# An FFT convolution and an MLP on one core: the filter loaded already turned, angle sums on GpSimd, fewer and wider shift matmuls, a new planned order

## The chip, the core and the metric

The kernel runs on one core of a Trainium2 chip. The metric is the device time of one execution in microseconds; several executions are run and the median is taken. The profiled execution is a single one of them, and its span is the time from its first to its last instruction.

TensorE (PE) multiplies, VectorE (DVE), ScalarE (ACT) and GpSimd (POOL) work on vectors, and SyncE (SP) issues most of the transfers (DMA). Each engine takes its instructions strictly in the order in which the program wrote them.

## The reference

Sequence length S = 2048, width D = 512, batch 1, bf16. A convolution block is followed by an MLP block, each with a residual. Layer norms have no weights.

```python
k_shift = sum over t of shift(k, 3 - t) * shift_k[:, t]       # 4 taps along the sequence
kv = k_shift * v
y  = irfft(rfft(kv, padded to 4096) * rfft(ssm_k, padded to 4096))[:2048] + kv * ssm_D
h  = q + layernorm(q) * y
# mixer and MLP on B = layernorm(h)
g  = gelu(layernorm(B) @ w1)              # then its four column groups move by -1, +1, -2, +2 rows
x1 = B + moved(g) @ w2
out = h + x1 + gelu(layernorm(x1) @ w3) @ w4    # w3: 512 x 1792, w4: 1792 x 512
```

## The kernel before

**Data.** Row `16 p + b` of the sequence lies in partition `p`, block `b` (16 blocks of 128 rows). The transforms of length 4096 are done as matmuls in two steps. A first small transform (`step1`, table `f1`) works on four blocks at once. Then an exchange over SBUF by DMA brings the rows together, and a second transform (`step2`, table `ftab`) follows for each of 16 frequency groups `kh`. Each group is multiplied by the filter's spectrum, transformed back (`inverse`), and sent over SBUF again; the last transform back (`inv1`) opens the MLP.

**Two plans.** The program is written as a list of tasks. A class `Plan` gives each task a cost on one or more engines, simulates them, tries 40 sets of priorities with random steps, and emits the best order it found. The numbers in it are a guess that sets the order and nothing else. There is one plan for the convolution and one for the MLP. Task names that are used below:

- `h`, `k`, `v`, `q`: loads of the filter (4 pieces), of k (4 pieces, transposed by the DMA), of v and of q (2 pieces of 1 MB each).
- `T`, `TE`: the filter comes as 512 x 2048 into `hnat`; `T` turns 128 x 128 pieces on PE, and `TE` copies them into `xh`. `dr` adds `ssm_D` to the filter's first row.
- `F`, `FE`, `FX`: first transform of the filter (tile `ph`, 16 tiles), its copy out of PSUM, and its exchange (L401, 16 transfers).
- `S`, `X`: the four shifted taps of k as matmuls against diagonal matrices `diag` (tile `pk`, 8 tiles of 128 x 1024), and the product with v on DVE (tile `xk`).
- `K`, `KE`, `KX`: first transform of kv (tile `pc`), its copy, its exchange (16 transfers).
- `G`, `GE`: second transform of the filter and its copy. `W`, `A`: second transform of kv (tile `pw`) and its copy. `P`: two products on DVE (L531, L532). `V`, `VE`, `VX`: transform back (tile `pv`), copy and exchange.
- `uu`, `an`, `sn`, `sg`, `tg`: the angles of the table `ftab` as integer sums, their wrap to 12 bits, the sines on ACT, signs, and the edges on POOL. `B`, `BE`: transposed tables for the way back. `diag`: the diagonal matrices, on POOL.
- `qs`, `qn`: statistics of q's rows for its layer norm (16 of them), and the power -1/2 on POOL.
- In the MLP: `I` is the last transform back (L598), `Y` scales it on ACT (L609), `H` forms h and its statistics on DVE (L620, L615), `W`, `X`, `M`, `O` are the four matmuls w1 to w4.

All PSUM tiles of the convolution come from one pool of four buffers (`big`): the n-th tile that PE fills waits until the tile four places ahead of it has been copied out. Copies out of PSUM (`FE`, `KE`, `GE`, `VE`) go to ACT or DVE, whichever the plan chose. All copies are written by one helper and so have line L321 (ACT) or L323 (DVE).

Of the kernel before, what the change touches and what calls it, by code (L numbers as in the profile page):

```python
# [34 lines left out]
class Plan:  # L35
# [26 lines left out]
    def forward(self, prio):  # L62
# [6 lines left out]
        while ready:  # L69
# [79 lines left out]
def kernel(  # L149
# [19 lines left out]
    KW = 16 + S  # L169

# [11 lines left out]
    hnat = view(ra, 0, DC * S, "p (c n) -> p c n", c=DC)  # L182
# [13 lines left out]
    ui = rt[:, 0:NK * 2 * 32].bitcast(I16)  # L196
# [14 lines left out]
    dum = const.tile([P, 1], F32, name="dum")  # L211
# [66 lines left out]
    a1 = small.tile([P, NK], I16, name="a1")  # L278
    b2i = small.tile([P, 2, 32], I32, name="b2i")
    b2 = small.tile([P, 2, 32], I16, name="b2")  # L280
# [27 lines left out]
    plan = Plan({"big": 4, "xk": 4, "asb": 3, "pr": 4, "vst": 5}, 40, {"V": 5.6, "A": 6.2, "G": 2.8, "PE": 5.5, "D": 1.8})  # L308
# [18 lines left out]

    def load(o, i, transpose=False):
        return lambda e: (nc.sync.dma_start_transpose if transpose else nc.sync.dma_start)(o, i)
# [10 lines left out]
    def angles(e):  # L340
        for r in range(2):
            nc.vector.tensor_tensor(out=uu[:, :, r, :, :],  # L342
                                    in0=a1[:].rearrange("p (k t) -> p k t", t=2).unsqueeze(3).to_broadcast([P, NH, 2, 32]),
                                    in1=b2[:, r, :].unsqueeze(1).unsqueeze(1).to_broadcast([P, NH, 2, 32]), op=ADD)
# [25 lines left out]
    task(("uu",), {"V": 2.4}, angles)  # L370
    task(("an",), {"V": 0.7}, wrap, [("uu",)])
    task(("sn",), {"A": 2.0}, sines, [("an",)])
    task(("sg",), {"V": 0.75}, signs, [("sn",)])
    task(("tg",), {"G": 2.3}, edges, [("sg",)])
    task(("diag",), {"G": 4.2}, taps, [("an",)])

    def turn(c, g):
        def f(e):
            pt = big(("pt", c, g), dt=BF16)
            for j in range(8):  # L380
                nc.tensor.transpose(pt[:, j, :], hnat[:, c, 8 * g + j:S:16], ident[:])
        return f

    def turned(c, g):
        return lambda e: copy(e, xh[:, 8 * g:8 * g + 8, c * P:(c + 1) * P], tl["pt", c, g])
# [9 lines left out]
    def out1(key, zc, bl, h):  # L395
        return lambda e: copy(e, zc[:, bl, h, :, :], tl[key][:])
# [7 lines left out]
    for g in range(2):  # L404
        for c in range(DC):
            task(("T", c, g), {"PE": 0.6}, turn(c, g), [("h", c)], take="big")
            task(("TE", c, g), {"A": 0.95, "V": 0.64}, turned(c, g), drop=("T", c, g))
    task(("dr",), {"V": 0.4}, lambda e: nc.vector.tensor_tensor(out=xh[0:1, 0, :], in0=xh[0:1, 0, :], in1=drow[:], op=ADD),
         [("TE", c, 0) for c in range(DC)])
    for bl in range(NL):  # L410
        for h in range(4):
            task(("F", bl, h), {"PE": 0.56}, step1(("ph", bl, h), lambda bq, bl=bl: xh[:, 4 * bl + bq, :], h),
                 [("TE", c, bl // 2) for c in range(DC)] + [("dr",)], take="big")
# [3 lines left out]
    def shift(p):  # L417
        def f(e):
            pk = big(("pk", p))
            for i in range(2):  # L420
                b = 2 * p + i
                for c in range(DC):
                    for j in range(4):
                        nc.tensor.matmul(pk[:, i, c * P:(c + 1) * P], lhsT=kT[:, c, 16 + b - j:KW - 16 + b - j + 1:16],  # L424
                                         rhs=diag[:, c, j, :], start=(j == 0), stop=(j == 3))
        return f

    def gated(p):
        def f(e):
            if p % 2 == 0:  # L430
                tl["xk", p // 2] = xkp.tile([P, 4, D], BF16, name="xk", tag="xk")
            nc.vector.tensor_tensor(out=tl["xk", p // 2][:, 2 * (p % 2):2 * (p % 2) + 2, :], in0=tl["pk", p][:],  # L432
                                    in1=v_sb[:, 2 * p:2 * p + 2, :], op=MUL)
        return f

    for p in range(NB // 2):
        task(("S", p), {"PE": 2.3}, shift(p), [("k", c) for c in range(DC)] + [("diag",)] + ([("S", p - 1)] if p else []), take="big")
        task(("X", p), {"V": 1.25}, gated(p), [("v", p // 4)] + ([("X", p - 1)] if p % 2 else []), take=None if p % 2 else "xk",
             drop=("S", p))
    for bl in range(NL):  # L440
        for h in range(4):
            task(("K", bl, h), {"PE": 0.56}, step1(("pc", bl, h), lambda bq, bl=bl: tl["xk", bl][:, bq, :], h),
                 [("X", 2 * bl + 1)], take="big", drop=("X", 2 * bl))
            task(("KE", bl, h), EV, out1(("pc", bl, h), zck, bl, h),
                 [("F", 3, 3)] if bl > 1 else [("T", c, 1) for c in range(DC)], drop=("K", bl, h))
# [58 lines left out]
    def qnorm(e):  # L504
        nc.gpsimd.tensor_scalar(out=qrs[:], in0=qmv[:, :, 1], scalar1=1e-5, scalar2=1.0, op0=ADD, op1=MUL)
        nc.gpsimd.tensor_tensor(out=qrs[:], in0=qrs[:], in1=mhalf[:, 0:1].to_broadcast([P, NB]), op=OP.pow)

    for b in range(NB):
        task(("qs", b), {"V": 0.85}, qstat(b), [("q", b // 8)])
    task(("qn",), {"G": 3.3}, qnorm, [("qs", b) for b in range(NB)])  # L510
    for kh in range(NH):
        task(("G", kh), {"PE": 0.56}, step2(("pg", kh), zh, kh), [("FX", bl) for bl in range(NL)] + [("tg",)], take="big")
# [5 lines left out]
    turns = {"asb": 0, "pr": 0, "vst": 0}  # L518
# [65 lines left out]
    plan = Plan({"mm": 6, "pt": 2, "lb": 6, "z": 4})  # L584
# [192 lines left out]

    for b in range(NB):
        if b % 4 == 0:
            task(("I", b // 4), {"PE": 2.45}, inv1(b // 4), take="mm", many=4)  # L780
        task(("Y", b), {"A": 0.72}, gate(b), take="z", drop=("I", b // 4), part=b % 4)
        task(("H", b), {"V": 1.6}, hsum(b), drop=("Y", b))
        if b % 2:
# [62 lines left out]
```

## Time and profile before

| what | value |
|---|---|
| median of 3 runs | 254.23 us (254.24, 254.23, 253.06) |
| profiled execution, its time | 252.79 us |
| its span | 251.0 us, mean granted clock 0.973 |
| busy: PE, DVE, ACT, POOL | 224.1, 165.0, 135.7, 54.0 us |
| instructions | 4538 |

The page of the profile has the busy share of each engine in 40 slices, the chain of work that ended last, the costliest groups of instructions and the transfers. Rows of a timeline give start, total duration, engine, line, operation, tile written and tiles read, the count, and in brackets the idle time ahead of it with what ended it. A duration is from an instruction's start to its end; neighbours overlap a little, so the pace of a row of equal instructions is a little shorter than one duration. Rows of windows give, after the stretch and its length, busy time and count for PE (and, where no engine is chosen, PE's weight loads, DVE, ACT and POOL), then the granted clock, the share of DMA and GB/s.

### The profile page before, as it was taken

Reading aid. Unit: us, or ns where it says so; the run is one execution under the profiler, and the core shown is the slowest. Engines: PE = TensorE matmul, PEld = TensorE weight load, DVE = VectorE, ACT = ScalarE, POOL = GpSimd, SP = SyncE. Lnnn points to the kernel's source line nnn. Section 1 sums busy time; section 2 is a strip of 40 time slices with the busy share of each in tenths; the row PEclk is TensorE's granted clock in tenths of the full one; section 3 lists DMA queues with packets and bytes.
Section 4 is the critical chain, followed back from the end, with each engine's and each line's share of the span. In section 5 each row is a group of like instructions: output and inputs, shape, how many; then the busy total and the mean of one; then the engine's idle time right before and its main releaser. Section 6 shows DMA issues by size and latency. Waiting matters only on the chain.

```text
span 251.0 us, 4538 instructions
## 1 busy us (share of the span) xinstructions
PE 224.1 (89%) x1803; PEld 118.6 (47%) x1803; DVE 165.0 (66%) x325; ACT 135.7 (54%) x191; POOL 54.0 (22%) x101
## 2 busy tenths in 40 slices
PE   8489998987988966388899999999999999999994
PEld 3446985443332322165567564454444444444441
DVE  7979899997997955999999947991222320015221
ACT  3567018877997995579379565567000067641000
POOL 3630000005010020699974522420000000000000
PEclk9959999999999999979799999999999999999999
DMA  6999980586245287900000000000011100000111
GB/s 219 263 237 411 376 341 4 230 356 252 102 139 198 101 264 242 379 7 4 0 0 3 0 1 3 1 0 0 24 42 42 42 24 0 0 21 24 42 42 42
DMA packets 18791, 28.08 MB, mean 112 GB/s; under 512 B 10065, under 2 KB 13906, under 8 KB 17234
## 3 DMA queue, kind: packets, MB, share of 16 engines
q1 hardware_dynamic: 17952, 26.74, 30.6%
q0 software_dynamic: 288, 1.05, 1.4%
q8 instruction: 14, 0.23, 0.4%
q10 hardware_dynamic: 530, 0.01, 0.1%
q14 instruction: 7, 0.06, 0.1%
HBM read 11.02 MB, written 2.10 MB: 52 GB/s over the span
## 4 chain that ended last, share of the span: by engine, by line
PE 58%; DVE 26%; ACT 5%; POOL 4%; DMA 3%; issue 2%; SPq 1%; ACTq 0%; POOLq 0%
PE mm L766 19%; PE mm L751 19%; PE mm L711 5%; PE pk L424 3%; DVE ra L323 3%; DVE qst L500 3%; DVE rd L620 3%; DVE st L615 3%; PE mm L686 2%; DVE xk L432 2%; DVE rt L342 2%; ACT rb L321 2%; DVE rb L531 2%; PE ptx L672 2%; DVE rb L532 2%
## 5 line engine op out<-in xcount | busy, mean ns | idle before, releaser
L757 ACT ACTIVATE ra<-mm 128x512 bf16<-128x512 f32 x56 | 33.4, 597 | 49.7 <-PE mm L751 49.6
L774 DVE TENSOR_TENSOR ob<-mm,rd 128x512 bf16<-128x512 f32 x16 | 11.1, 692 | 61.4 <-PE mm L766 61.4
L751 PE MATMUL mm<-rc,rb 128*128 128x512 bf16 x224 | 50.8, 379 | 0.0
L766 PE MATMUL mm<-rt,ra 128*128 128x512 bf16 x224 | 49.0, 379 | 0.0
L766 PEld LDWEIGHTS <-ra 128*128 128x128 bf16 x224 | 21.9, 98 | 26.4
L751 PEld LDWEIGHTS <-rb 128*128 128x128 bf16 x224 | 21.7, 98 | 24.8
L321 ACT CAST rc<-ph 128x1024 bf16<-128x1024 f32 x11 | 10.8, 1025 | 15.0 <-PE ph L392 15.0
L541 PE MATMUL pv<-rb,rt 64*128 64x512 bf16 x128 | 16.6, 378 | 2.0 <-DVE rd L323 1.3
L686 PE MATMUL mm<-rc,rf 128*128 128x256 bf16 x128 | 17.8, 294 | 0.0
L711 PE MATMUL mm<-rf,rb 128*128 128x512 bf16 x64 | 16.9, 391 | 0.4 <-ACT rb L692 0.3
L321 ACT CAST rb<-pw 128x1024 bf16<-128x1024 f32 x16 | 16.2, 1027 | 2.1 <-PE pw L454 1.4
L424 PEld LDWEIGHTS <-rb 128*128 128x128 bf16 x256 | 16.3, 149 | 1.5 <-issue 1.5
L424 PE MATMUL pk<-diag,rb 128*128 128x128 bf16 x256 | 16.6, 226 | 0.3 <-ACT ra L321 0.3
L321 ACT COPY rc<-ptx 128x512 bf16<-128x512 bf16 x26 | 14.7, 587 | 3.9 <-PE ptx L672 3.9
L620 DVE SCALAR_TENSOR_TENSOR rd<-q_sb,qmv,z 128x512 bf16<-128x512 bf16 x16 | 12.7, 791 | 6.0 <-ACT z L609 6.0
L716 DVE SCALAR_TENSOR_TENSOR q_sb<-rd,cr,mm 128x512 bf16<-128x512 bf16 x16 | 11.7, 734 | 4.2 <-PE mm L711 4.2
L686 PEld LDWEIGHTS <-rf 128*128 128x128 bf16 x128 | 13.2, 106 | 2.2
L692 ACT ACTIVATE rb<-mm 128x512 bf16<-128x512 f32 x16 | 9.5, 610 | 7.4 <-PE mm L711 5.3
L609 ACT ACTIVATE z<-mm,qrs 128x512 f32<-128x512 f32 x16 | 10.6, 697 | 4.4 <-PE mm L598 2.7
L321 ACT CAST rb<-pv 128x1024 bf16<-128x1024 f32 x12 | 12.1, 1039 | 1.3 <-PE pv L541 1.3
L454 PEld LDWEIGHTS <-rf 128*64 128x64 bf16 x128 | 6.6, 108 | 13.0 <-issue 9.4
L640 POOL TENSOR_TENSOR rr<-uw,mhalf 128x4 f32<-128x4 f32 x8 | 10.4, 1296 | 10.3 <-DVE hm L629 10.3
(128 smaller groups left out, 333.7 us busy)
## 6 DMA issues: line engine op xcount, KB each, us to landing
rd<-rc SPq DMA_DIRECT2D x16, 256.0 KB, 4.9
rc<-ra SPq DMA_DIRECT2D x16, 256.0 KB, 3.4
ra<-rb SPq DMA_DIRECT2D x16, 256.0 KB, 2.7
ra<-in_A_ssm_k_dram SPq DMA_DIRECT2D x4, 512.0 KB, 5.2
q_sb<-in_A_q_dram SPq DMA_DIRECT2D x2, 1024.0 KB, 7.7
rb<-in_A_v_dram SPq DMA_DIRECT2D x2, 1024.0 KB, 10.6
out_dram<-ob SPq DMA_DIRECT2D x16, 128.0 KB, 1.8
rb<-in_B_w_dram SPq DMA_DIRECT2D x1, 1792.0 KB, 7.0
```

The source lines that it names most:

```text
L321: nc.scalar.copy(o, i)
L424: nc.tensor.matmul(pk[:, i, c * P:(c + 1) * P], lhsT=kT[:, c, 16 + b - j:KW - 16 + b - j + 1:16], rhs=diag[:, c, j, :], start=(j == 0), st ...
L541: nc.tensor.matmul(ps[:, t, :], lhsT=tt[hs, min(x, 2), kh, :], rhs=pr[hs, x // 2, x % 2, :], start=(x == 0), stop=(x == 3))
L609: nc.scalar.activation(z[:], tl["y", b][:], ACT.Identity, bias=1.0, scale=qrs[:, b:b + 1])
L620: nc.vector.scalar_tensor_tensor(out=h_sb[:, b, :], in0=q_sb[:, b, :], scalar=qmv[:, b, 0:1], in1=tl["z", b][:], op0=SUB, op1=MUL)
L686: nc.tensor.matmul(pw_[:, j * 256:(j + 1) * 256], lhsT=w1_sb[:, k, m * P:(m + 1) * P], rhs=hnT[:, k, p * 256:(p + 1) * 256], start=(k == 0 ...
L711: nc.tensor.matmul(px[:], lhsT=shifted(m, b), rhs=w2_sb[:, m, :], start=(m == 0), stop=(m == DC - 1))
L716: nc.vector.scalar_tensor_tensor(out=x1[:, b, :], in0=hbm[:, b, :], scalar=tl["cr", b // 2][:, b % 2:b % 2 + 1], in1=tl["x", b][:], op0=MU ...
L751: nc.tensor.matmul(pg[:], lhsT=w3_sb[:, k, fc * P:(fc + 1) * P], rhs=lnT[:, k, g * 512:(g + 1) * 512], start=(k == 0), stop=(k == DC - 1))
L757: nc.scalar.activation(gbuf[:, g % 2, fc, :], tl["g", g, fc][:], ACT.Gelu_apprx_tanh)
L766: nc.tensor.matmul(po[:], lhsT=gbuf[:, g % 2, fc, i * P:(i + 1) * P], rhs=w4_sb[:, fc, :], start=(fc == 0), stop=(fc == FC - 1))
L774: nc.vector.tensor_tensor(out=ob[:], in0=tl["o", 4 * g + i][:], in1=xh1[:, b, :], op=ADD)
```

## The change

- The host hands the filter over turned and laid out as 128 x 16 x 512; it is loaded straight into `xh`. `T` and `TE` are gone.
- All twelve loads are issued in one written order: the filter's four pieces, k 0 and 1, v 0 and 1, q 0, k 2 and 3, q 1.
- The angle sums `uu` move from DVE to POOL and to int32, behind two copies of 8 columns into `dumg`, which wait for the tables `f1` and `s0`. The wrap (now int32) and the sines are written behind the fourth copy that DVE makes of `ph`, the signs and edges behind the fifth.
- `S` is cut by four blocks and two column groups: 14 matmuls of 128 to 512 columns into one tile, against 32 of 128 columns.
- Ten statistics of q stay in the convolution's plan, six move to the front of the MLP's, with a second power on POOL.
- Dummy matmuls `wm` on zeros: three tiles at the end of the first plan, behind VE 13 to 15, and four in the second, behind H 2 to 5.
- The planner frees a tile that has no reader, tries 150 sets of priorities in place of 40, and has smaller PE costs; a task `in` of 3.4 stands ahead of `I`.

```diff
-    ui = rt[:, 0:NK * 2 * 32].bitcast(I16)
+    ui = rt[:, 0:NK * 4 * 32].bitcast(I32)
...
-    for c in range(DC):
-        task(("h", c), {"D": 1.45}, load(hnat[:, c, :], A_ssm_k[c * P:(c + 1) * P, :]), lat=LAND, rank=60)
+    for bl in range(NL):
+        task(("h", bl), {"D": 1.45}, load(xh[:, 4 * bl:4 * bl + 4, :], A_ssm_k[:, 4 * bl:4 * bl + 4, :]), lat=LAND, rank=60)
...
     def angles(e):
-        for r in range(2):
-            nc.vector.tensor_tensor(out=uu[:, :, r, :, :],
+        for r in range(-2, 2):
+            if r < 0: nc.gpsimd.tensor_copy(dumg[:], (f1[:, 3, 1, 24:32], s0[:, 1, 1, 24:32])[r]); continue
+            nc.gpsimd.tensor_tensor(out=uu[:, :, r, :, :],
...
     def out1(key, zc, bl, h):
-        return lambda e: copy(e, zc[:, bl, h, :, :], tl[key][:])
+        def f(e):
+            copy(e, zc[:, bl, h, :, :], tl[key][:])
+            if e == "V" and key[0] == "ph":
+                turns["rc"] = turns.get("rc", 0) + 1
+                for g in {4: (wrap, sines), 5: (signs, edges)}.get(turns["rc"], ()):
+                    g(e)
+        return f
...
-            pk = big(("pk", p))
+            pk = big(("pk", bl, ch))
             for i in range(2):
-                b = 2 * p + i
-                for c in range(DC):
-                    for j in range(4):
-                        nc.tensor.matmul(pk[:, i, c * P:(c + 1) * P], lhsT=kT[:, c, 16 + b - j:KW - 16 + b - j + 1:16],
-                                         rhs=diag[:, c, j, :], start=(j == 0), stop=(j == 3))
+                c = 2 * ch + i
+                for m in (0, -3, -2, -1, 1, 2, 3):
+                    lo, hi, x = max(0, -m), min(3, 3 - m), 16 + 4 * bl + m
+                    nc.tensor.matmul(pk[:, i, P * (m + lo):P * (m + hi + 1)], lhsT=kT[:, c, x:x + S - 15:16],
+                                     rhs=diag[:, c, lo:hi + 1, :].rearrange("p j x -> p (j x)"), start=(m == 0), stop=(m == 3))
...
-    for b in range(NB):
+    for b in range(NQ):                      # NQ = 10
         task(("qs", b), {"V": 0.85}, qstat(b), [("q", b // 8)])
...
+    for kh in range(NH - 3, NH):
+        task(("wm", kh), {"PE": 0.87}, warm, [("VE", kh)], take="big", rank=-10)
+    for n in (0, 1, 2, 3, 4, 5, 8, 9, 10, 6, 7, 11):
+        loads[n]()
...
+    task(("in",), {"D": 3.4}, lambda e: None)
+    for b in range(NQ, NB):
+        task(("qs", b), {"V": 0.85}, qstat(b), rank=20)
+    task(("qn",), {"G": 1.7}, qnorm(NQ, NB), [("qs", b) for b in range(NQ, NB)])
...
+        if 1 < b < 6:
+            task(("wm", b), {"PE": 0.87}, warm(b), [("H", b)], take="mm", rank=-100)
...
+        if name == "A_ssm_k":
+            a = _np.ascontiguousarray(a.T.reshape(P, NB, D))
```

DVE, from the angle table `u0k` to the first statistics of q, before:

```order
L303 TENSOR_SCALAR u0k<-u0k 128x128
L342 TENSOR_TENSOR rt<-a_161,b_163 128x16x64 x2
L323 COPY ra<-pt 128x8x128
L347 TENSOR_SCALAR rt<-rt 128x2048
L323 COPY ra<-pt 128x8x128 x3
L408 TENSOR_TENSOR ra<-ra,drow 1x512
L353 TENSOR_SCALAR rf<-rf,sgo 128x64x32
L323 CAST rc<-ph 128x1024 x5
L500 BN_STATS qst<-q_sb 128x6
```

and after the change (`rt` holds the angles, `rf` the table, `ra` the filter, `rc` its first transform):

```order
L305 TENSOR_SCALAR u0k<-u0k 128x128
L407 TENSOR_TENSOR ra<-ra,drow 1x512
L325 CAST rc<-ph 128x1024 x4
L353 TENSOR_SCALAR rt<-rt 128x2048
L325 CAST rc<-ph 128x1024
L359 TENSOR_SCALAR rf<-rf,sgo 128x64x32
L432 TENSOR_TENSOR xk<-pk,rb 128x4x256 x3
```

The sums and the four copies of turned pieces have left DVE; the added row is its first work on data, and the wrap stands behind four copies of F and ahead of the fifth.

POOL, from its last small constant to the edges of the table, before:

```order
L251 MEMSET u0p 128x1
L366 TENSOR_TENSOR diag<-ident,ssk_bf 128x2048
L356 TENSOR_SCALAR rf<-s_181,pf 128x2x32
L357 TENSOR_SCALAR rf<-s_181,pf 128x2x32
L358 COPY t_72<-rf 128x2x127
```

and after:

```order
L253 MEMSET u0p 128x1
L347 COPY dumg<-f_70 128x8
L347 COPY dumg<-s_182 128x8
L348 TENSOR_TENSOR rt<-a_162,b_164 128x16x64 x2
L372 TENSOR_TENSOR diag<-ident,ssk_bf 128x2048
L362 TENSOR_SCALAR rf<-s_182,pf 128x2x32
```

Two small copies and the two sums now stand ahead of the diagonal matrices. SP's queue of loads, as one piece of the difference:

```order
-L329 DMA ra<-in_A_ssm_k_dram 128x2048 x4
-L329 DMA_TRANSPOSE rb<-in_A_k_dram 128x2048 x4
-L329 DMA q_sb<-in_A_q_dram 128x4096
-L329 DMA rb<-in_A_v_dram 128x4096
+L333 DMA ra<-in_A_ssm_k_dram 128x2048 x4
+L333 DMA_TRANSPOSE rb<-in_A_k_dram 128x2048 x2
+L333 DMA rb<-in_A_v_dram 128x4096 x2
+L333 DMA q_sb<-in_A_q_dram 128x4096
+L333 DMA_TRANSPOSE rb<-in_A_k_dram 128x2048 x2
```

The second half of k's transposed pieces now stands behind both pieces of v and the first of q.

More of the change, by code (lines that the diff above doesn't have):

```diff
@@ L96, in forward @@
                     gone[m, i] = done[n] + t["lat"]
+            if t["take"] and not any(t["users"]):
+                gone.update({(n, i): done[n] for i in range(t["many"])})
             ready.remove(n)
@@ L368, in taps @@
                                 in1=ssk_bf[:].rearrange("p c j -> p (c j)").unsqueeze(2).to_broadcast([P, 16, P]), op=MUL)
[L370 to L374, printed above, removed]
-    task(("diag",), {"G": 4.2}, taps, [("an",)])
[L377 to L385, printed above, removed]
+    task(("uu",), {"G": 5.0}, angles)
+    turns = {"asb": 0, "pr": 0, "vst": 0}
+    task(("an",), {"V": 2.2}, lambda e: None, [("uu",)])
+    task(("sn",), {"A": 2.0}, lambda e: None, [("an",)])
+    task(("sg",), {"V": 0.75}, lambda e: None, [("sn",)])
+    task(("tg",), {"G": 2.3}, lambda e: None, [("sg",)])
+    task(("diag",), {"G": 4.2}, taps, [("an",)])
     def step1(key, xs, h):
@@ L440 @@
+    for bl in range(NL):
+        for ch in range(2):
+            task(("S", bl, ch), {"PE": 1.78}, shift(bl, ch), [("k", 2 * ch), ("k", 2 * ch + 1), ("diag",)], take="big")
+            task(("X", bl, ch), {"V": 1.25}, gated(bl, ch), [("v", bl // 2)] + ([("X", bl, 0)] if ch else []), take=None if ch else "xk",
+                 drop=("S", bl, ch))
     for bl in range(NL):
         for h in range(4):
[L442 to L443 removed]
+            task(("K", bl, h), {"PE": 0.45}, step1(("pc", bl, h), lambda bq, bl=bl: tl["xk", bl][:, bq, :], h),
+                 [("X", bl, 1)], take="big", drop=("X", bl, 0))
```

79 lines of the change are left out of this document (43 added, 36 removed).

## The prediction

> **What bounds the kernel now.** I read the chain first, then the windows of TensorE, then each engine's timeline over the first 60 us, because the change touches mostly the convolution stage there.
>
> ```profile
> PE 58%; DVE 26%; ACT 5%; POOL 4%; DMA 3%; issue 2%; SPq 1%; ACTq 0%; POOLq 0%
> 5.66 5.68 DVE rt L342 x2
> 14.64 3.63 PE ph L392 x32
> 22.52 8.16 PE pk L424 x128
> 57.59 0.64 PE pw L454 x4
> 91.09 3.46 DMA ra<-rb
> 131.00:141.00 10.00, 9.69 (x85) 6.73 (x84) 9.55 (x23) 7.24 (x14) 4.92 (x9) 1.00 0.01 2
> ```
>
> From about 131 us PE is busy 9.69 of 10, so the MLP gains nothing except by an earlier start. Before 94.55 (91.09 + 3.46, where the last filtered tile lands) the chain runs through DVE, PE and ACT in turn. It opens with 5.68 us of angle sums on DVE (L342), and F (the first transform of the filter, `ph`) starts only at 14.64. W, which opens the products, starts at 57.59.
>
> ```profile
> L342 DVE TENSOR_TENSOR rt<-a,b x2: 1219/2924/4629, 5.6 to 6.7; 128x1024 int16<-128x1024 int16 x2
> 6.41 3.85 POOL L366 TENSOR_TENSOR diag<-ident,ssk_bf 128x2048 bf16<-128x2048 bf16 x1 [3.63 <-DMA ssk_bf<-in_A_shift_k_dram]
> 5.43 0.23 DVE L303 TENSOR_SCALAR u0k<-u0k 128x128 int32<-128x128 int32 x1
> 3.83 0.20 DVE L288 TENSOR_SCALAR u1k<-u1k 128x64 int32<-128x64 int32 x1
> 11.86 0.68 DVE L347 TENSOR_SCALAR rt<-rt 128x2048 int16<-128x2048 int16 x1
> 14.50 0.40 DVE L408 TENSOR_TENSOR ra<-ra,drow 1x512 bf16<-1x512 bf16 x1
> 5.75 0.40 ACT L305 ACTIVATE s<-u0k,negpi 128x128 bf16<-128x128 int32 x1 [1.28 <-DVE u0k L303]
> 12.57 2.01 ACT L350 ACTIVATE rf<-rt,negpi 128x2048 bf16<-128x2048 int16 x1 [2.64 <-DVE rt L347]
> 115.09 0.72 DVE L635 TENSOR_SCALAR uw<-hv 128x2 f32<-128x2 f32 x2
> 114.27 1.52 POOL L660 TENSOR_SCALAR rd<-rd,rr,hm 128x512 bf16<-128x512 bf16 x2
> ```
>
> One angle sum took 1.22 us, its twin 4.63: it began at 6.71 and ended at 11.34, 1.08 after POOL's `diag` ended at 10.26. DVE was held for as long as POOL worked. At 115.09 even two tiny one-source operations stretched to 0.72, to the end of a POOL operation (115.79).
>
> ```profile
> 8.66:12.07 3.41, 0.30 (x6) 0.98 1.15 194
> 12.07:15.49 3.42, 2.64 (x28) 0.50 1.24 249
> 15.49:18.90 3.41, 3.41 (x40) 0.52 1.14 230
> 117.89:121.31 3.42, 1.49 (x15) 0.98 0.00 0
> 121.31:124.72 3.41, 3.41 (x16) 0.52 0.00 0
> ```
>
> After a window of 3.41 us with 0.30 us of PE work the clock is granted at 0.5 for two windows; after one with 1.49, for one (the column behind PE's count is the clock).
>
> **The change, part by part.** *Start of F.* The 64 transposes with their eight copies go, since the filter arrives turned. F needs only the first load and the added row (L408, 0.40), which now follows `u0k` (ends 5.66): F starts at 6.1 instead of 14.64. The four loads keep their bytes and their place at the head of SP's queue, so their price stays:
>
> ```profile
> ra<-in_A_ssm_k_dram SPq DMA_DIRECT2D x4, 512.0 KB, 5.2
> ```
>
> The exchanges stand behind all twelve loads on SP, as before. The planner's own edits and the turning of the filter on the host cost the chip nothing. The two new 8-column copies on POOL wait for `s0` (ends 6.15), so POOL's sums start near 6.35, behind that row's 0.40, and do not hold it.
>
> *Angles.* POOL adds 2 x 1024 int32 elements. No row shows that; the nearest is `diag`, 2048 bf16 elements in 3.85. As low end I take DVE's free price, 2 x 1.22, as high end twice `diag` (four bytes for two), 7.7; I take 3.85, the same engine and operation. So the sums end at 10.2, and `diag`, next on POOL with its data there, runs to 14.05. The Trainium skill ("GPSIMD Engine Reference", 3.1 Elementwise — side-by-side cycle accounting) gives 4497 ns for a tensor add of 2048 fp32 on GpSimd; by this estimate of 4.5 the total would come 0.65 later, 249.7.
>
> ```profile
> 45.45 3.48 DVE L323 CAST ra<-pc 128x1024 bf16<-128x1024 f32 x3
> 46.76 4.76 ACT L321 CAST ra<-pc 128x1024 bf16<-128x1024 f32 x5 [0.28 <-ACT ra L321]
> 14.64 7.88 PE L392 MATMUL ph<-ra,f 128*32 128x512 bf16 x96 [0.78 <-DVE ra L323]
> 47.82 1.53 PE L392 MATMUL pc<-xk,f 128*32 128x512 bf16 x24 [0.24 <-ACT ra L321]
> 50.57 0.61 PE L463 MATMUL tb<-ident,rf 128*128 128x128 bf16 x8
> 22.45 12.21 PE L424 MATMUL pk<-diag,rb 128*128 128x128 bf16 x192
> 138.40 1.73 PE mm L711 x8
> 41.78 2.15 PE L424 MATMUL pk<-diag,rb 128*128 128x128 bf16 x32 [0.30 <-ACT ra L321]
> 51.77 1.01 ACT L321 CAST ra<-pc 128x1024 bf16<-128x1024 f32 x1 [0.26 <-PE pc L392]
> ```
>
> *To the first shift S.* DVE makes four copies of F's tiles (3.48/3 = 1.16 each) from 7.3 to 11.9 (F's second tile is ready two times 7.88/12 = 0.6 after 6.1), then comes the wrap. It is int32 now: 64 more elements cost 0.03 (0.23 - 0.20), so 2048 cost 1.15; the int16 row, 0.68, is the low end, twice 1.15 the high one. It reads one SBUF operand; I take it as held like the rows above, until `diag` ends at 14.05, so it is done at 15.2. The sines (2.01) end at 17.2. On ACT they stand ahead of the copies of F's tenth and eleventh tile, two of 4.76/5 = 0.95, ended at 19.1. PSUM has four buffers, S's first tile is the fourteenth and needs the tenth's: S starts at 19.2, before at 22.45. Gain 3.2. `k` loads 0 and 1, issued first as before, must land by then.
>
> *Shift.* Same 4096 columns a tile, 14 matmuls instead of 32. Before, 12.21/6 = 2.03 a tile; 4096 columns in matmuls of 512 took 1.73 (L711), which are the two bounds. The four 128-wide ones still take 12.21/192 = 0.064 where 0.054 would do, so 1.77. To the end of the last S the new order has 8 S (14.2), five F or K tiles (1.53/3, 2.5 together) and four tables (0.55 each, 2.2): 19.2 + 18.9 = 38.1. PE will have stood from 12.9 to 19.2, over a window, so it runs S at half clock for a window or two: 1.7 to 3.4 lost less what falls into the wait; I take 1.6. Last S ends at 39.7, before at 43.93: gain 4.2.
>
> *To W.* One product X (1.2, as the old tiles' rate) and six K copies (7.0) on DVE end at 47.9. Before, the last K copy ended at 52.78 on ACT and W came 4.8 later, behind sixteen exchanges; the same 4.8 gives 52.7, gain 4.9. Six of the sixteen q statistics no longer stand in this stretch.
>
> ```profile
> 23.01 0.68 DVE L500 BATCH_NORM_STATS2 qst<-q_sb 128x6 f32<-128x512 bf16 x1
> 23.82 0.66 DVE L500 BATCH_NORM_STATS2 qst<-q_sb 128x6 f32<-128x512 bf16 x1
> 96.96 0.75 DVE L620 SCALAR_TENSOR_TENSOR rd<-q_sb,qmv,z 128x512 bf16<-128x512 bf16 x1 [5.96 <-ACT z L609]
> 57.28 2.94 POOL L506 TENSOR_TENSOR qrs<-qrs,mhalf 128x16 f32<-128x16 f32 x1
> ```
>
> *Statistics.* Each takes 23.82 - 23.01 = 0.81; six are 4.9, put into the 5.96 for which DVE waited before 96.96. They cost nothing, with 1.1 of cover to spare; without cover, up to 4.9. POOL's second power is at most 2.94 beside waiting engines.
>
> *W to the landing.* Kept at 94.55 - 57.59 = 37.0; one of three dummy tiles stands ahead of the last V on PE, 0 to 0.9, taken as 0.7. Landing at 90.4: gain 4.2.
>
> *MLP.* The window 121.31 lost 3.41 x 0.48 = 1.6 with PE full. Four dummy tiles among the H rows should keep the clock; they cost 4 x 0.87 of PE where PE waits for DVE. They also put transposes behind H.2 to H.5 in PE's queue. Bounds: gain 1.6, loss 0.6 (one dummy not hidden less nothing won back); I take a gain of 1.0.
>
> *Sum.* 4.2 + 1.0 = 5.2. The profiled execution took 252.79 (span 251.0): 247.6. The median shown, 254.23, is 1.4 above it, and I take the sum off the median: 249.0.
>
> **Rivals.** *The wrap is not held, and PE stays warm:* wrap at 11.9 to 13.05, sines 15.05, S at 17.1, 2.1 earlier, and 1.6 of slow clock gone: 245.3. For it: no row shows a one-source operation of this length against POOL; against it: 115.09. The Trainium skill ("SBUF — State Buffer", SBUF: two separate sides) says that a DVE operation in a two-port mode and a GpSimd one exclude each other for the whole instruction; by that rule the wrap is held, as forecast, and the 4.63 of L342 agrees.
>
> *Cold longer:* S loses 3.4 instead of 1.6, and the dummies win nothing (1.0): 251.8. For it: the two windows from 12.07, and PE still has gaps before W.
>
> ```profile
> GB/s 219 263 237 411 376 341 4 230 356 252 102 139 198 101 264 242 379 7 4 0 0 3 0 1 3 1 0 0 24 42 42 42 24 0 0 21 24 42 42 42
> L329 SPq DMA_TRANSPOSE rb<-in_A_k_dram x4: 2156/2538/6104, 2.6 to 13.5; - x4
> DMA to landing us min/median/max: 5.2/6.2/9.2
> ```
>
> *Late `k`:* loads 2 and 3 now stand in SP's queue behind three of 1 MB. SP has issued k1 by 2.6 + 6.1 + 2.5 = 11.2; the three take 7.5 at 400 GB/s, and two more transposing issues of 2.5 follow, so k3 should land near 27, 30 at worst (9.2 from its issue). S.1.1 needs it at 31.6 (19.2 + 4 S, three F, four tables, slow clock). From 31.6 on each microsecond late costs one; landing at 36 gives 253.4, no change.
>
> *Slower: int32 on POOL.* If the sums go by a slower routine, each microsecond over 3.85 moves `diag`, wrap, sines and S alike. At 7.7 the time is 252.9; it decides against the change from 10.4 for the pair (5 ns an element against `diag`'s 1.88): 255.5 and more. No row excludes it.
>
> **How the numbers follow.** Forecast 0.46, its own range 247.3 to 250.7; not held or warm 0.20; cold longer 0.17; late `k`, or a gain lost in the exchanges alike, 0.07; slow integers 0.10, half of it near 252.9 and half above 255.5. Half a per cent, 1.3 us, is about what a measurement of this kernel tells from no change: faster means under 252.96. Forecast, not held, cold and a part of the 7.7 case make 0.84; same 0.10; slower 0.06. The range 245.2 to 253.0 leaves out half of the second case and the upper ones.
>
> **What would show it.** F's first matmul near 6.1; POOL's two sums near 3.85 in all; the wrap with a duration of 3 us or a gap before it, ending near 15.2; S from 19.2 with a row of 1.8 a tile once warm, and a clock row of 0.5 in it; last S 39.7; W 52.7; landing 90.4; six statistics in DVE's wait before the first H with H not later than 2.4 after the landing; no half clock between W1 and the first M. I am wrong if S starts before 18 or after 21, or if PE waits for `k` in S.1.1.

## The result, and the profile after

The changed kernel takes 242.55 us (median of 12 runs, 241.19 to 243.10 but for one), the kernel before 253.40 (15 runs): a ratio of 0.957, 95% interval 0.954 to 0.960. Forecast were 249.0 and a range of 245.2 to 253.0: the direction was right, the gain of 10.9 us twice the forecast 5.2. The one slow run, of 323.44 us at a mean granted clock of 0.661, was the one first profiled, so all rows of "after" here are from the same kernel profiled again beside the first experiments (span 240.9; its 4 runs have a median of 242.07).

Its chain by engine, from the page; before, PE had 58% and DVE 26%:

```profile
PE 55%; DVE 31%; ACT 5%; DMA 2%; issue 2%; POOL 2%; SPq 1%; POOLq 1%; ACTq 0%; DVEq 0%
```

The timeline of the first stage, row by row in the order in which the forecast walked through it (start, duration, engine, line, tiles, in brackets the idle time ahead and its releaser); the last row, apart, is from the chain and ends the stage:

```profile
6.04 5.71 PE L389 MATMUL ph<-ra,f 128*32 128x512 bf16 x88 [0.82 <-DVE ra L407]
6.43 3.79 POOL L348 TENSOR_TENSOR rt<-a,b 128x1024 int32<-128x1024 int32 x2
10.18 3.61 POOL L372 TENSOR_TENSOR diag<-ident,ssk_bf 128x2048 bf16<-128x2048 bf16 x1
7.37 4.78 DVE L325 CAST rc<-ph 128x1024 bf16<-128x1024 f32 x4 [1.39 <-PE ph L389]
12.07 2.80 DVE L353 TENSOR_SCALAR rt<-rt 128x2048 int32<-128x2048 int32 x1
14.79 1.21 DVE L325 CAST rc<-ph 128x1024 bf16<-128x1024 f32 x1
14.90 2.00 ACT L356 ACTIVATE rf<-rt,negpi 128x2048 bf16<-128x2048 int32 x1 [3.02 <-DVE rt L353]
16.81 2.82 ACT L323 CAST rc<-ph 128x1024 bf16<-128x1024 f32 x3
16.14 8.15 PE L423 MATMUL pk<-diag,rb 128*128 128x512 bf16 x42 [3.16 <-DVE rc L325]
21.17 1.22 DVE L432 TENSOR_TENSOR xk<-pk,rb 128x1024 bf16<-128x1024 f32 x1 [3.48 <-DMA rb<-in_A_v_dram]
36.09 2.00 PE L423 MATMUL pk<-diag,rb 128*128 128x512 bf16 x14
50.05 1.49 PE L456 MATMUL pw<-rc,rf 128*64 128x512 bf16 x12 [0.90 <-DMA rc<-ra]
```
```profile
82.48 3.56 DMA ra<-rb
```

| point | before | forecast | after | gap |
|---|---|---|---|---|
| F's first matmul | 14.64 | 6.1 | 6.04 | |
| wrap done | 12.54 | 15.2 | 14.87 | |
| sines done | 14.58 | 17.2 | 16.90 | |
| S starts | 22.45 | 19.2 | 16.14 | 3.1 earlier |
| last S ends | 43.93 | 39.7 | 38.09 | 1.6 earlier |
| W | 57.59 | 52.7 | 50.05 | 2.6 earlier |
| last tile landed | 94.55 | 90.4 | 86.04 | 4.4 earlier |
| span | 251.0 | 245.8 | 240.9 | 4.9 shorter |

Up to the sines every step came within 0.35 of the forecast. Then S starts 3 us too early, and the row says why: it waits for DVE's copy of F (L325, which ends at 16.00), not for ACT's copies behind the sines (16.81 on), for which the forecast made it wait.

### The profile page after: what moved, and what is told of

Same layout as the page of the kernel before. It is cut to its first block, busy times and chain, and to the rows that moved or that the text cites. A ratio compares the mean times of both kernels' runs of the same rounds, so it can differ in the third digit from the quotient of the medians.

```text
span 321.7 us, 4184 instructions
## 1 busy us (share of the span) xinstructions
PE 313.9 (98%) x1623; PEld 134.0 (42%) x1623; DVE 159.1 (49%) x317; ACT 137.4 (43%) x194; POOL 51.5 (16%) x102
## 3 DMA queue, kind: packets, MB, share of 16 engines
q0 software_dynamic: 288, 1.05, 1.0%
## 4 chain that ended last, share of the span: by engine, by line
PE 90%; DVE 7%; POOL 1%; issue 0%; ACT 0%; ACTq 0%; DVEq 0%; POOLq 0%
PE mm L778 23%; PE mm L763 23%; PE pv L544 7%; PE pk L423 7%; PE mm L723 6%; PE mm L698 6%; PE pw L456 3%; PE pg L456 3%; PE pc L389 3%; PE ptx L684 3%; PE ph L389 2%; DVE st L627 2%; PE mm L610 2%; DVE rd L632 2%; DVE rc L325 1%; PE wm L562 1%
## 5 line engine op out<-in xcount | busy, mean ns | idle before, releaser
L763 PE MATMUL mm<-rc,rb 128*128 128x512 bf16 x224 | 75.1, 512 | 0.0
L778 PE MATMUL mm<-rt,ra 128*128 128x512 bf16 x224 | 73.5, 512 | 0.0
L778 PEld LDWEIGHTS <-ra 128*128 128x128 bf16 x224 | 27.2, 121 | 45.9 <-issue 45.9
L723 PE MATMUL mm<-rf,rb 128*128 128x512 bf16 x64 | 23.0, 512 | 0.0
L423 PE MATMUL pk<-diag,rb 128*128 128x256 bf16 (+3 forms) x112 | 21.6, 369 | 1.3 <-DVE rc L325 1.3
L544 PE MATMUL pv<-rb,rt 64*128 64x512 bf16 x128 | 22.6, 490 | 0.0
L698 PE MATMUL mm<-rc,rf 128*128 128x256 bf16 x128 | 22.1, 348 | 0.0
L432 DVE TENSOR_TENSOR xk<-pk,rb 128x1024 bf16<-128x1024 f32 x8 | 9.8, 1225 | 9.4 <-PE pk L423 6.9
L323 ACT CAST ra<-pc 128x1024 bf16<-128x1024 f32 x10 | 9.8, 1014 | 8.2 <-PE pc L389 8.2
L610 PE MATMUL mm<-ra,f 32*128 32x512 bf16 x128 | 12.0, 502 | 1.4 <-ACT z L621 1.2
```

The source lines that it names most:

```text
L323: nc.scalar.copy(o, i)
L423: nc.tensor.matmul(pk[:, i, P * (m + lo):P * (m + hi + 1)], lhsT=kT[:, c, x:x + S - 15:16], rhs=diag[:, c, lo:hi + 1, :].rearrange("p j x ...
L544: nc.tensor.matmul(ps[:, t, :], lhsT=tt[hs, min(x, 2), kh, :], rhs=pr[hs, x // 2, x % 2, :], start=(x == 0), stop=(x == 3))
L610: nc.tensor.matmul(ys[bq][:], lhsT=f2[hs, x, :], rhs=wv[hs, bl, x // 2, x % 2, :], start=(x == 0), stop=(x == 7))
L698: nc.tensor.matmul(pw_[:, j * 256:(j + 1) * 256], lhsT=w1_sb[:, k, m * P:(m + 1) * P], rhs=hnT[:, k, p * 256:(p + 1) * 256], start=(k == 0 ...
L723: nc.tensor.matmul(px[:], lhsT=shifted(m, b), rhs=w2_sb[:, m, :], start=(m == 0), stop=(m == DC - 1))
```

## The experiments

All are run beside the kernel before, and the ratio is to its runs of the same batch. "Against after" compares with 242.4, the median of 15 runs of the changed kernel (241.2 to 243.8), across batches in which the kernel before had medians of 253.57 to 254.09: medians less than 1 us apart are not told apart by these times.

| run | median (range) us | ratio to before, 95% | against after |
|---|---|---|---|
| the change itself | 242.07 (241.72 to 243.79) | 0.956 [0.950, 0.961] | |
| buffers in strict turn | 244.79 (244.47 to 245.14) | 0.965 [0.959, 0.971] | +2.4 |
| six statistics early | 246.21 (245.64 to 246.76) | 0.971 [0.966, 0.976] | +3.8 |
| no dummies | 244.45 (243.61 to 245.21) | 0.963 [0.959, 0.968] | +2.0 |
| no MLP dummies | 242.92 (242.04 to 243.37) | 0.957 [0.953, 0.960] | +0.5 |
| old shift | 243.08 (242.19 to 243.31) | 0.958 [0.953, 0.963] | +0.7 |
| sums on VectorE | 242.83 (241.95 to 242.99) | 0.956 [0.952, 0.960] | +0.4 |
| before + turned filter | 250.80 (248.46 to 252.58) | 0.985 [0.979, 0.991] | |
| wrap later | 242.30 (240.84 to 244.42) | 0.954 [0.950, 0.959] | -0.1 |
| k turned | 241.23 (239.53 to 242.05) | 0.949 [0.945, 0.953] | -1.2 |
| wrap later and k turned | 237.66 (237.06 to 238.33) | 0.936 [0.933, 0.940] | -4.7 |

**The change itself**, for the profile above.

> The changed kernel as it stands, for an undisturbed profile of it. Theory 1 (the early stage): the first shift tile S starts near 16.1, not 19.2, because PE takes the PSUM buffer that was released first and not the one four tiles back; PE then idles about 1 us, no half clock follows, the last S ends near 35, W near 48, the landing near 85.5; the MLP from the landing takes 154 to 155. Theory 2 (the MLP): the landing is near 90 as predicted, and the MLP from there is 5 to 6 us shorter than before because the dummy matmuls keep the clock.

S's start (16.14) and the length of the MLP (154.9) came as its first theory says. But PE stood 3.16 us ahead of S and a half clock did follow, so the last S ended at 38.09 and W came at 50.05, not near 35 and 48.

**Which buffer S gets.** In the built program the pool hands out the buffer whose last reader was written first, and not the one four tiles back, as the description of the kernel before has it. S's first tile so gets the buffer of F's twelfth tile, which is DVE's fifth copy; the forecast took the buffers in turn, which is the tenth's, copied by ACT behind the sines. The run forces that turn for every tile of the convolution:

```diff
-    ps_a = p0.enter_context(tc.tile_pool(name="ps_a", bufs=4, space=PSUM))
+    ps_a = p0.enter_context(tc.tile_pool(name="ps_a", bufs=1, space=PSUM))
...
-        t = ps_a.tile([P, 2, D], F32, name=key[0], tag="big")
+        t = ps_a.tile([P, 2, D], F32, name=key[0], tag="big%d" % (slot[0] % 4))
+        slot[0] += 1
```

> Same order of work, but the four PSUM buffers of the convolution are four separate tags taken in strict turn, so that S's first tile must wait for the copy of the tenth F tile, which stands behind the sines on ACT. Theory 1: S starts at 18.5 to 19.5 instead of near 16.1, a window of half clock follows, and the time is 3 to 6 us over the changed kernel (246 to 248.5), close to the 249.0 that was forecast. Theory 2: the early stage has slack, at most 1 us more.

Two rows of its timeline, PE and ACT:

```profile
18.80 7.61 PE L425 MATMUL pk<-diag,rb 128*128 128x512 bf16 x42 [5.68 <-POOL rf L365]
16.80 2.82 ACT L325 CAST rc<-ph 128x1024 bf16<-128x1024 f32 x3
```

The tenth tile's copy is the second of the three and ends at 18.71, and S starts at 18.80: the forecast's 19.2, within 0.4. (The releaser named there, a POOL operation, had ended at 18.4.) W comes at 51.79 and the landing at 88.24. The handing out of buffers is worth 2.7 beside the change in the same batch, 2.4 against all its runs, a little under the 3 to 6 that were expected.

**The six statistics.** They are put back into the convolution, right behind the tenth:

```diff
+            if b == NQ - 1:
+                for x in range(NQ, NB):
+                    qstat(x)(e)
```

> Same order, but the six statistics of q's rows 10 to 15 are issued on DVE right behind the tenth one in the convolution instead of ahead of the MLP. Theory 1: DVE is on the path from the last S to W, so nearly all of 6 x 0.81 = 4.9 us comes back, 3.5 to 5 us slower. Rival: DVE waits there for PE anyway and the move is worth under 1.5 us.

A row of PE's timeline, then two windows (length, PE busy and count, ..., granted clock, DMA share, GB/s):

```profile
43.12 4.89 PE L389 MATMUL pc<-xk,f 128*32 128x512 bf16 x56 [2.85 <-DVE xk L432]
```
```profile
39.38:42.79 3.41, 0.61 (x8) 0.12 (x7) 3.29 (x8) 1.14 (x2) 0.18 (x1) 1.00 0.52 216
42.79:46.20 3.41, 3.08 (x36) 1.42 (x40) 3.41 (x4) 1.74 (x2) 0.00 (x0) 0.62 0.68 269
```

DVE does statistics up to 41.9 while PE stands and waits for DVE's last X; the clock then drops. W moves to 53.29, the time by 3.8, inside the 3.5 to 5 that were expected. In the changed kernel the same six run behind DVE's last product, as these rows of DVE show:

```profile
86.55 0.18 DVE L503 BATCH_NORM_AGGREGATE qmv<-qst 128x2 f32<-128x6 f32 x1
88.45 0.75 DVE L632 SCALAR_TENSOR_TENSOR rd<-q_sb,qmv,z 128x512 bf16<-128x512 bf16 x1 [1.71 <-ACT z L621]
```

They end 1.7 before H needs DVE, and H comes 2.41 after the landing, as before the change (96.96 - 94.55). Of the parts of the change that were undone, this one is worth most.

**The dummies.** First all seven tiles issue nothing, then only the four in the MLP; the plan keeps its order.

```diff
-        task(("wm", kh), {"PE": 0.87}, warm, [("VE", kh)], take="big", rank=-10)
+        task(("wm", kh), {"PE": 0.87}, lambda e: None, [("VE", kh)], take="big", rank=-10)
...
-            task(("wm", b), {"PE": 0.87}, warm(b), [("H", b)], take="mm", rank=-100)
+            task(("wm", b), {"PE": 0.87}, lambda e: None, [("H", b)], take="mm", rank=-100)
```

> Same order, but the seven dummy matmul tiles issue nothing. Theory 1: they are worth at most the 1.6 us of one half-clock window in front of the MLP, and without them PE's queue is shorter: between 1.0 faster and 1.6 slower than the changed kernel. Theory 2: 4 to 6 us slower, with one or two windows at 0.5 between the landing and 30 us behind it.

> Only the four dummy tiles among the H rows issue nothing; the three at the end of the products stay. Theory (the three keep the clock for the last transform back, worth the 1.0 us by which the first H came later without any dummies; the four keep it between 94 and 108): first H at 88.4 as with all, a half-clock window near 98 to 108, 0.7 to 1.4 slower, 242.8 to 243.5. Rival (only the three matter): 242.1. Rival (only the four matter): 244.4.

Without any, three windows and DVE's first H:

```profile
80.34:83.75 3.41, 2.06 (x16) 0.43 (x11) 3.34 (x8) 2.96 (x4) 0.66 (x2) 1.00 0.84 255
83.75:87.16 3.41, 2.17 (x20) 0.58 (x24) 2.64 (x8) 1.25 (x2) 0.45 (x2) 0.65 0.54 208
97.40:100.82 3.42, 1.56 (x12) 1.12 (x13) 3.28 (x9) 3.33 (x6) 3.12 (x5) 0.65 0.18 64
```
```profile
89.43 0.75 DVE L632 SCALAR_TENSOR_TENSOR rd<-q_sb,qmv,z 128x512 bf16<-128x512 bf16 x1 [2.90 <-ACT z L621]
```

The time moves by 2.0, between the two theories. The landing stays (85.98 against 86.04), so the three dummies ahead of it cost nothing. Without them the last transform back starts at half clock, and H comes 3.45 after the landing instead of 2.41. With the three kept and only the four left out:

```profile
97.40:100.82 3.42, 1.05 (x8) 0.87 (x9) 3.28 (x10) 3.00 (x6) 3.13 (x5) 0.50 0.12 41
100.82:104.23 3.41, 3.32 (x24) 2.75 (x24) 3.27 (x10) 2.35 (x4) 3.18 (x8) 0.57 0.01 2
```

Two windows at or near half clock, and the time moves by 0.5, which the runs don't tell from nothing: in the first of them DVE is busy 3.28 of 3.42 and PE 1.05, so a slower PE costs little there. So the three earn about 1.5 of the 2.0 and the four at most the rest.

**The shape of the shift** goes back to 32 matmuls of 128 columns a tile:

```diff
-                for m in (0, -3, -2, -1, 1, 2, 3):
-                    lo, hi, x = max(0, -m), min(3, 3 - m), 16 + 4 * bl + m
...
+                for b in range(4):
+                    for j in range(4):
+                        x = 16 + 4 * bl + b - j
+                        nc.tensor.matmul(pk[:, i, P * b:P * b + P], lhsT=kT[:, c, x:x + S - 15:16],
+                                         rhs=diag[:, c, j, :], start=(j == 0), stop=(j == 3))
```

> Only the shift's shape goes back: 32 matmuls of 128 columns a tile instead of 14 of 128 to 512, the same 4096 columns and the same order of tasks. Theory (S is on the path from its start to W): a warm tile takes 2.03 instead of 1.8, so 8 tiles 1.8 to 2.0 more, W near 52, 244. Rival (PE is not what ends last between S and W, loads or DVE's X and copies are): W moves by under 0.5, 242 to 242.5.

Three tiles at full clock here, and then the start of W; in the changed kernel the same three took 5.50:

```profile
29.34 6.14 PE L424 MATMUL pk<-diag,rb 128*128 128x128 bf16 x96
50.09 1.49 PE L457 MATMUL pw<-rc,rf 128*64 128x512 bf16 x12 [0.44 <-DMA rc<-ra]
```

A tile is 0.21 dearer, 1.7 for eight. The last S ends only 0.5 later (38.59), because one window of S was at half clock in this profile and about two in the changed kernel's. W stands where it stood (50.09, 50.05), and the time moved by 0.7, within the spread. The shape is worth something between 0 and 1.

**The angle sums.** Both go back to DVE in int16, behind the added row, with the int16 wrap (a run with int32 sums on DVE gave no result):

```diff
-    ui = rt[:, 0:NK * 4 * 32].bitcast(I32)
+    ui = rt[:, 0:NK * 2 * 32].bitcast(I16)
...
-            if r < 0: nc.gpsimd.tensor_copy(dumg[:], (f1[:, 3, 1, 24:32], s0[:, 1, 1, 24:32])[r]); continue
-            nc.gpsimd.tensor_tensor(out=uu[:, :, r, :, :],
+            if r < 0: continue
+            nc.vector.tensor_tensor(out=uu[:, :, r, :, :],
```

> Only the angles go back: both sums on DVE in int16, right behind the added row, and the int16 wrap in its place behind DVE's fourth copy. Theory (DVE is held for as long as POOL works, and F's copies stand behind the sums): diag runs on POOL from 6.4 to 10.2, the second sum ends near 11.3, DVE's four copies near 16, the wrap (0.7, free) near 16.7, the fifth copy near 17.9, and S starts there instead of at 16.1; with PE idle longer up to 1 us more: 244 to 245. Rival (the sums aren't held where no transposes wait, and the move to POOL only bought a held wrap): sums done at 8.4, S starts at 15, 241.

```profile
5.90 2.34 DVE L348 TENSOR_TENSOR rt<-a,b 128x1024 int16<-128x1024 int16 x2
6.79 4.92 POOL L372 TENSOR_TENSOR diag<-ident,ssk_bf 128x2048 bf16<-128x2048 bf16 x1 [4.03 <-DMA ssk_bf<-in_A_shift_k_dram]
14.76 5.51 PE L427 MATMUL pk<-diag,rb 128*128 128x512 bf16 x41 [1.21 <-DVE rc L325]
20.19 3.49 DVE L436 TENSOR_TENSOR xk<-pk,rb 128x1024 bf16<-128x1024 f32 x3 [3.89 <-DMA rb<-in_A_v_dram]
```

My theory was wrong here. The sums run free, each in 1.21; it is `diag` that is held until they end: it ends at 11.71, 3.5 behind them. S starts at 14.76, 1.4 earlier than with the sums on POOL, and nothing comes of it: X waits 3.89 for v, and the time is the same. W comes at 49.38, 0.7 earlier, but its first twelve matmuls are at half clock and take 2.52 instead of 1.49. The move to POOL bought nothing that can be measured.

**The turned filter alone**, put into the kernel before; its planner then made an order of its own:

```diff
-        task(("h", c), {"D": 1.45}, load(hnat[:, c, :], A_ssm_k[c * P:(c + 1) * P, :]), lat=LAND, rank=60)
+        task(("h", bl), {"D": 1.45}, load(xh[:, 4 * bl:4 * bl + 4, :], A_ssm_k[:, 4 * bl:4 * bl + 4, :]), lat=LAND, rank=60)
...
-            task(("T", c, g), {"PE": 0.6}, turn(c, g), [("h", c)], take="big")
-            task(("TE", c, g), {"A": 0.95, "V": 0.64}, turned(c, g), drop=("T", c, g))
```

> The kernel before with one part of the change alone: the filter handed over turned and loaded straight, its 64 transposes and eight copies gone. Theory (the angle sums on DVE hold the start of F, not the transposes): the added row stands behind the sums and the wrap, F starts near 12.4 instead of 14.6, DVE's copies of F wait for nothing else, S starts at 21 to 22 instead of 22.45: 0 to 1.5 won, 252 to 253.5. Rival (the transposes were the cost): F at 6, S at 16 to 18, 246 to 248.

```profile
7.96 3.98 DVE L346 TENSOR_SCALAR rt<-rt 128x2048 int16<-128x2048 int16 x1
13.45 0.61 PE L381 MATMUL ph<-ra,f 128*32 128x512 bf16 x8 [3.26 <-DVE rc L322]
21.51 14.12 PE L409 MATMUL pk<-diag,rb 128*128 128x128 bf16 x224
```

It won 1.5% (0.9 to 2.1), about 3 us, more than the 0 to 1.5 us expected and less than the rival's. F's first tiles did not wait for the added row (only those of the first four blocks need it), but after seven of them PE stood 3.3 us: DVE's copies came behind a wrap that `diag` held for 3.98 instead of 0.68. S started only 0.9 earlier than before; the landing came 1.5 earlier (93.06), and the other 1.4 of this profile was won behind it. By these rows an early F reaches S only where the copies of F stand ahead of the wrap, as in the new order. No run tests that, and none tests the new order of the tasks or of the loads by itself.

**What S's start is worth, and what is late next.** Two edits, alone and together: the wrap behind DVE's fifth copy of F instead of the fourth, and k handed over turned, so that its four transposing loads become plain ones.

```diff
-                for g in {4: (wrap, sines), 5: (signs, edges)}.get(turns["rc"], ()):
+                for g in {5: (wrap, sines, signs, edges)}.get(turns["rc"], ()):
...
-        task(("k", c), {"D": 2.25}, load(kT[:, c, 16:KW], k_r[:, c * P:(c + 1) * P], True), lat=LAND, rank=10)
+        task(("k", c), {"D": 2.25}, load(kT[:, c, 16:KW], A_k[c * P:(c + 1) * P, :]), lat=LAND, rank=10)
...
+        if name == "A_k":
+            a = _np.ascontiguousarray(a[0].T)
```

> Only the wrap and the sines move: they are written behind DVE's fifth copy of an F tile instead of the fourth. Theory (S waits for a PSUM buffer that DVE's fifth copy frees, and that copy stands behind the held wrap): the fifth copy now ends near 13.3, the wrap is free of diag (1.2 instead of 2.8), and S starts at 13.9, behind diag (ends 13.8), instead of 16.1. PE then stands for 0.9 instead of 3.2, so no half clock in S. The fourth PSUM tile behind it still needs X's product, which needs v (landed at 21.2): F.3.0 at 22.5 instead of 24.2, so 1.7 won, 240.3. Rival (the loads bind from here on): S.1.1, which needs the last two pieces of k, starts at 29.8 as before with a wait for a DMA ahead of it, and nothing is won, 242.1. Second rival (S waits for k 1, not for a buffer): S still starts at 16.

> The changed kernel with k handed over turned, the wrap where the change put it (behind DVE's fourth copy). Theory (two limits that cover each other: S's buffer behind the held wrap, and the loads): S still starts at 16.1 behind DVE's fifth copy and at half clock, X no longer waits for v (lands before 17), and of the 4.4 us that both edits won together only 1.5 to 2.5 come: 239.6 to 240.6. Rival (the loads alone bind): 237.7 as with both edits. Second rival (they only bind with an earlier S): 242.

> As e4, and k is handed over already turned, so that its four pieces are plain loads of the same bytes. If the loads bind (v at 21.2, k 2 and 3 later): v lands before 19, X follows the first S tile, PE goes through S without a stop, last S ends near 34 instead of 38.1, W near 46 instead of 50.0, time 237.5 to 238.5. If they don't bind: as e4, about 240.3. If only the order on PE and DVE binds from S to W: as e4 too.

With the wrap later, three rows of PE and one of its chain:

```profile
15.28 4.38 PE L423 MATMUL pk<-diag,rb 128*128 128x128 bf16 x34 [0.41 <-DMA rb<-in_A_k_dram]
22.18 0.61 PE L389 MATMUL ph<-ra,f 128*32 128x512 bf16 x8 [0.52 <-DVE xk L432]
48.44 1.49 PE L456 MATMUL pw<-rc,rf 128*64 128x512 bf16 x12 [2.15 <-DMA rc<-ra]
```
```profile
12.04 7.64 DMA rb<-in_A_v_dram
```

S starts at 13.83, behind `diag`, as expected, with the clock whole, and W comes 1.6 earlier in this profile, which is of the fastest of 6 runs. But now the loads bind: PE waits for k, DVE for v, PE for X, and in the median of the 6 runs nothing is left of the 1.7 expected. With k turned alone, X waits for PE instead of v:

```profile
16.14 1.31 PE L422 MATMUL pk<-diag,rb 128*128 128x512 bf16 x7 [3.08 <-DVE rc L324]
19.19 1.22 DVE L431 TENSOR_TENSOR xk<-pk,rb 128x1024 bf16<-128x1024 f32 x1 [1.51 <-PE pk L422]
```

That is the other limit: S still waits for its buffer. It wins 1.2, where 239.6 to 240.6 was expected and 241.23 came. With both edits neither holds:

```profile
17.87 3.49 DVE L431 TENSOR_TENSOR xk<-pk,rb 128x1024 bf16<-128x1024 f32 x3 [0.19 <-DMA rb<-in_A_v_dram]
45.05 1.49 PE L455 MATMUL pw<-rc,rf 128*64 128x512 bf16 x12 [0.59 <-DMA rc<-ra]
```

W comes 5.0 earlier, and the time is 237.66, as expected and the best of all kernels here: 0 and 1.2 alone, 4.7 together. In the changed kernel two limits stood almost at the same place. An edit to one of them shows the other one. With the sums on VectorE and S at 14.76 the row of X shows the same wait for v; that this alone kept the time was not tested.

## Why the prediction was wrong, point by point

- **F's start, POOL's sums, `diag`, the held wrap, the sines**: right, each within 0.35 (3.79 for the sums where 3.85 was taken; the wrap 2.80 long, ended 1.08 after `diag`). In the run with the wrap later, behind the end of `diag` at 13.78, the same wrap is free and takes 1.22:

```profile
14.00 1.22 DVE L353 TENSOR_SCALAR rt<-rt 128x2048 int32<-128x2048 int32 x1
```

  The rivals "not held" and "slow integers" are out. The estimate of 4.5 for the sums, which goes by the fp32 figure of the Trainium skill ("GPSIMD Engine Reference", 3.1 Elementwise — side-by-side cycle accounting), was high by 0.7 for this integer pair.
- **"PSUM has four buffers, S's first tile is the fourteenth and needs the tenth's"**: the step that failed. The count of buffers was right and the turn was not: S got the twelfth tile's buffer, which DVE's fifth copy freed at 16.00, and started at 16.14 instead of 19.2. Forced into turn, S started at 18.80, and the gap to the forecast time shrank by 2.7.
- **Half clock in S**: foreseen, and by chance larger in this profile than was taken. The granted clock in the changed kernel's profile:

```profile
12.07:15.48 3.41, 0.91 (x16) 0.27 (x8) 3.41 (x3) 0.58 (x1) 1.72 (x1) 0.91 1.06 302
15.48:18.90 3.42, 2.75 (x11) 1.68 (x12) 1.27 (x2) 3.42 (x4) 1.04 (x4) 0.50 1.01 383
18.90:22.31 3.41, 3.41 (x18) 2.23 (x17) 1.14 (x1) 0.73 (x1) 1.13 (x5) 0.59 1.30 350
```

  About two windows: the first three tiles of S took 8.15 instead of 5.50, 2.65 lost where 1.6 was taken, and from S's start to the last S's end it took 21.95 instead of 20.5. This error of 1.45 went the other way and, by these points, hid part of the first. In four of the six profiles in which S starts at 16.14 only one window was slow. The run without dummies is one of them:

```profile
16.14 7.14 PE L423 MATMUL pk<-diag,rb 128*128 128x512 bf16 x42 [3.22 <-DVE rc L325]
```

  Its last S ends at 37.08, 1.0 earlier, but its W comes at 49.85, only 0.2 earlier. By these two profiles, what the clock loses in S reaches W in part at most.
- **Last S to W**: 11.96 where 13.0 was taken. The 4.8 from the last K copy to W became 3.5: the last exchange landed in 2.37 (47.55 to 49.92 in the chain) instead of 3.48.
- **W to the landing, 37.0 kept and 0.7 for a dummy**: 35.99. The 0.7 for a dummy is nothing (the run without dummies took 36.13). The other 1.0 wasn't tested by itself. The rows offer a reason that is not shown to be the cause: 36 matmuls of G stand behind W instead of 44, so two tiles fewer are left for PE and the copying engines.
- **Six statistics at no cost**: right, with 1.7 of cover left (1.1 forecast); without it 3.8 (up to 4.9 forecast).
- **Dummies in the MLP, gain 1.0**: the stretch from the landing to the end became 1.6 shorter (154.9 against 156.45; without any dummies 156.7), and no half-clock window stands between W1 and the first M. But the four bring about 0.5 at most. The three at the end of the products, priced as a cost, keep the clock for the last transform back and are worth about 1.5 against a kernel without them.
- **Late `k`**: no wait in S.1.1. The loads show elsewhere: v for X, at 21.17, behind S's first tile.
- **The base**: the forecast set the median 3.2 above the span (249.0 - 245.8), since the three times shown had a median 1.4 above the profiled execution. The changed kernel's median is 1.6 above its profiled span.

The sum of it, by the points of this one profile: 3.1 too late a start of S, less 1.45 in S, plus 1.0 before W, 1.7 after W, 0.5 in the MLP: 4.9 on the span; with 1.6 in the base it is the 6.5 between 249.0 and 242.55. I was to be wrong "if S starts before 18", and it did. As to what made the 11 us: undone one by one, the statistics gave back 3.8, the dummies 2.0, the shift and the sums under 1 each, and the turned filter alone won 3; these parts overlap and were measured on two bases, so they are not a sum. The 2.4 of the buffers is no part of the change, since the kernel before takes its tiles from the same pool. What the new order is worth by itself stays open.

## What to carry to other kernels

A wait for a buffer is priced only when it is known whose buffer the pool hands out; that is read from the built program, or the price is given for each candidate. When an edit removes a stall and nothing moves, look for a second limit at the same place (here v and k on the DMA queue) and remove both in one run before the first is called worthless. Statistics or other work without a deadline belongs behind the last operation that another engine waits for.

## What the runs showed of the hardware

- **A hold goes both ways.** Before, `diag` started on POOL at 6.41 and DVE's second sum at 6.71, and the sum took 4.63. With the sums on VectorE `diag` started at 6.79 and the second sum at 7.04, but here the sum took 1.21, and `diag` 4.92 instead of 3.6. With the turned filter alone the second sum started at 6.70, ahead of `diag`, and `diag` was stretched:

```profile
5.57 2.35 DVE L341 TENSOR_TENSOR rt<-a,b 128x1024 int16<-128x1024 int16 x2
7.00 4.39 POOL L365 TENSOR_TENSOR diag<-ident,ssk_bf 128x2048 bf16<-128x2048 bf16 x1 [4.23 <-DMA ssk_bf<-in_A_shift_k_dram]
```

  The Trainium skill ("SBUF — State Buffer", SBUF: two separate sides) says that whichever starts first has the shared ports for the whole instruction and the other is blocked. The third case agrees. In the first two `diag` had started by its row while the first sum still ran, 0.30 and 0.25 us ahead of the second sum, and it went first only once; the rows do not show why. One long duration in one profile can thus be a coin that fell that way.
- **The clock was lost to stops shorter than a window.** PE stops of 2.35 (no dummies, before the last transform back), 2.85 (statistics early) and 3.16 us (ahead of S) were each followed by one or two windows at half clock. Ahead of W a stop of 2.23 (sums on VectorE) made the first twelve matmuls take 2.52, and one of 2.15 (wrap later) left them at 1.49. The Trainium skill ("TensorE: Matmul & The Clock Gate", Part 1: The HAM clock gate (the "warmup" mystery)) speaks of at least one idle window of about 3.4; here less was enough. The length of the stop does not settle how much is lost: ahead of S it was 3.08 to 3.27 in six profiles, and about two slow windows followed in two of them (the changed kernel, no MLP dummies) and one in the other four.
- **Transposing loads hold their queue.** SP's rows for k, the first two and the last two pieces in the changed kernel, then the last two with k turned, plain loads of the same bytes:

```profile
2.68 8.41 SPq L333 DMA_TRANSPOSE rb<-in_A_k_dram  x2
12.71 13.04 SPq L333 DMA_TRANSPOSE rb<-in_A_k_dram  x2
```
```profile
7.12 1.17 SPq L332 DMA_DIRECT2D rb<-in_A_k_dram  x2
```

  21.5 us of issuing became 2.3. The exchange of F, which stands behind all loads on SP, starts at 12.26 instead of 26.50:

```profile
26.50 13.41 SPq L404 DMA_DIRECT2D rd<-rc  x16
```
```profile
12.26 23.64 SPq L403 DMA_DIRECT2D rd<-rc  x16
```

  In the GB/s rows of the two pages (40 slices of 6 us), the changed kernel's and then that with k turned, the second to fourth slice moved 418 to 426 instead of 271 to 336:

```profile
GB/s 199 271 336 295 233 389 373 321 380 91 131 220 113 234 186 396 120 4 0 3 0 1 3 0 0 3 1 0 44 46 44 44 0 0 3 0 44 44 44 44
```
```profile
GB/s 204 418 422 426 197 353 112 357 326 89 131 242 112 244 190 400 93 3 0 3 0 1 3 0 0 3 1 0 44 47 44 44 0 0 3 0 44 44 44 44
```
